# A one-scalar minimum on GpSimd, written with a second scalar

## The chip, the core and the metric

The kernel runs on one core of one Trainium2 chip. The metric is the device time of one execution in microseconds (us), as the median of several runs. Engines are named as in the profile: PE is TensorE's matmuls, PEld its weight loads, DVE VectorE, ACT ScalarE, POOL GpSimd, SP SyncE (here the queue that issues nearly all DMAs).

## What is computed

A chain of three layers in float32, on 4 batches of 576 tokens:

1. attention of 8 heads of width 64, mixed by a gate with a lookup in a memory matrix:

```python
scores = q @ k.T / 8, causal;  local = softmax(scores) @ v
phi(x) = where(x > 0, x, exp(x) - 1.0) + 1.0
mem_out = (phi(q) @ M_prev) / (phi(q) @ z_prev + 1e-6)
x = g * mem_out + (1 - g) * local          # g = sigmoid(beta), per head
```

2. `x @ w_in`, then `h - tanh(h)`, then `@ w_out` (512 to 2048 to 512), over 2304 tokens;
3. a second such layer (512 to 1024 to 512) with softmax and a layer norm between its two products.

The change lies in `phi`, the feature map. The kernel computes it as max(x + 1, exp(min(x, 0))), which is the same function.

## The kernel before

The program has three stages on one time axis. **Attention** works on 16 pairs of heads (`p` = 0 to 15), from the start to about 200 us. **Moe1** is the second item above, in eight slices of 256 hidden columns by five blocks of tokens, to about 580 us. **Moe2** is the third, in 18 tiles of 128 tokens, to the end.

The order of the attention stage is written out by hand. A table of text (`PROLOGUE` for the first pairs, then `PERIOD` with two halves, one for each parity of `p`) names one small step after another, as `f_neg:-1:p` for "step `f_neg`, of the pair one behind, on GpSimd". `run` issues them in just this order, and each engine executes its own steps in the order of issue. An engine whose next step has to wait stands still, with all that is queued behind it. Two pairs of heads thus take one turn of the table.

The steps that the prediction speaks of, by line:

- `q_t`, `k_t` (L248), DVE: transposes of q and k. They wait for the q and k loads on SP's queue (L187).
- `f_neg` (L263), POOL: `e` = min(qT, 0), a tile of 128 partitions by 576 elements, two buffers. Its input is the transposed q.
- `f_exp` (L266), ACT: exponential of `e`; `f_max` (L270), DVE: max(qT + 1, `e`), which makes `f`.
- `m_mm` (L282), PE: `f` times the memory matrix, into `R`; `m_mul` (L301), DVE: `R` divided, into `xm`.
- `s_r` (L326) and `s_l` (L342), PE: scores `S` and, for the last 64 rows of two pairs together, `S_L`; `s_max` (L356), DVE; `s_exp` (L383), ACT: the exponentials `P` and `PL` and their sums `sm`.
- `s_eps` (L395), POOL: 1e-9 added to a few sums, one scalar; `s_inv` (L399), DVE: their reciprocals.
- `s_norm` (L410), POOL: each block of `P` and `PL` times its reciprocal and the gate, two scalars taken from memory.
- `a_t` (L450), PE: transposes `T` of the blocks of `P`, and last in a turn those of `PL` (the shared last rows); `a_ev` (L457), ACT, copies them out; `a_mem` (L432) and `a_pv` (L477), PE: the products with v, `X`.
- between them, POOL also prepares the next stage: `split_x` (L675), from pair 4 on, and the conversion of weights (L887, L896).

In Moe1, L890 on POOL is one more operation of two scalars: a product with a value from memory, and a product with the constant 1.0.

The step that the change touches, and what runs the table:

Of the kernel before, what the change touches and what calls it, by code (L numbers as in the profile page):

```python
# [13 lines left out]
ALU = mybir.AluOpType  # L14
# [17 lines left out]
class Attention:  # L32
# [227 lines left out]

    def f_neg(self, p):
        e = self.e[p] = self.sp.tile([P, self.S], F32, tag="fe", name=f"e{p}", bufs=2)
        self.eng.tensor_scalar_min(e, self.QT[p], 0.0)  # L263

    def f_exp(self, p):
        self.nc.scalar.activation(self.e[p], self.e[p], AF.Exp)  # L266
# [1043 lines left out]
```

## Time and profile before

| | |
|---|---|
| median of 3 runs | 788.77 us (788.38 to 789.33) |
| the profiled execution's own time | 789.29 us |
| its span, first to last instruction | 787.5 us |
| PE, share of the span | 99% |
| DVE, POOL, ACT | 72%, 48%, 44% |
| granted TensorE clock | full in all 40 slices of the span |

The profile shows one execution. Its span is 1.8 us shorter than its own time. Busy PE is modelled (matmuls overlap, and their ends are reckoned), so 99% tells little of whether PE waited; what the text uses are starts of groups of matmuls on the time axis, and the waits of the weight loads ahead of them.

### The profile page before, as it was taken

The numbers are of one execution on the slowest core, as the hardware profiler recorded it, in microseconds if no ns is written. First come the engines' busy times: TensorE is split into PE (matmuls) and PEld (weight loads), VectorE is DVE, ScalarE is ACT, GpSimd is POOL, SyncE is SP. The second block draws the span as 40 slices with busy tenths as digits, with TensorE's granted clock in tenths as the row PEclk, the third lists the DMA queues.
The fourth block names the chain that finished last, engine by engine and source line by source line (L and its number), as shares of the span: only waits on it lengthen the run. The fifth ranks groups of instructions, "written<-read, shape, count | busy, mean of one in ns | idle before, by whom it ended". The sixth has DMA issues, their size and how long they took to land.

```text
span 787.5 us, 12510 instructions
## 1 busy us (share of the span) xinstructions
PE 777.2 (99%) x4532; PEld 645.9 (82%) x4532; DVE 567.7 (72%) x1064; ACT 348.5 (44%) x692; POOL 379.8 (48%) x386
## 2 busy tenths in 40 slices
PE   8999999999999999999999999999999999999998
PEld 6777677777798898988989889898898888888887
DVE  5899888983477786776877776777877766566661
ACT  4889899994243243242332422233322333323321
POOL 6788999986223342333333333334532443334421
PEclk9999999999999999999999999999999999999999
DMA  7677877651002221211212111112100344333341
GB/s 181 150 192 160 164 145 163 139 121 58 0 28 81 64 71 54 81 54 54 81 54 80 54 54 54 54 54 81 55 28 30 123 146 143 110 118 111 131 134 55
DMA packets 77119, 73.04 MB, mean 93 GB/s; under 512 B 51072, under 2 KB 60032, under 8 KB 77056
## 3 DMA queue, kind: packets, MB, share of 16 engines
q1 hardware_dynamic: 76896, 71.93, 34.0%
q8 instruction: 36, 0.59, 0.3%
q10 hardware_dynamic: 160, 0.30, 0.2%
q14 instruction: 27, 0.22, 0.1%
HBM read 54.38 MB, written 13.11 MB: 86 GB/s over the span
## 4 chain that ended last, share of the span: by engine, by line
PE 74%; DMA 1%; ACT 0%; DVE 0%; SPq 0%; issue 0%; ACTq 0%
PE Y L739 25%; PE H L707 24%; PE H L933 12%; PE O16X L1027 1%; PE O15S L1027 1%; PE O14X L1027 1%; PE O13X L1027 1%; PE O12X L1027 1%; PE O11X L1027 1%; PE O10X L1027 1%; PE O9X L1027 1%; PE O8X L1027 1%; PE O7X L1027 1%; PE O6X L1027 1%; PE O5X L1027 1%; PE O4X L1027 1%
## 5 line engine op out<-in xcount | busy, mean ns | idle before, releaser
L739 PE MATMUL Y<-G,wo 128*128 128x512 f32 (+1 forms) x960 | 204.8, 368 | 0.9 <-DVE G L724 0.6
L739 PEld LDWEIGHTS Y<-G,wo 128*128 128x128 f32 x960 | 174.6, 188 | 25.9 <-issue 1.6
L707 PE MATMUL H<-xh,wi 128*128 128x512 f32 (+1 forms) x640 | 151.6, 369 | 0.0
L887 POOL TENSOR_TENSOR raw<-raw,cva 128x512 f32<-128x512 f32 x48 | 63.0, 1313 | 174.6 <-DVE cva L885 161.0
L707 PEld LDWEIGHTS H<-xh,wi 128*128 128x128 f32 x640 | 117.1, 188 | 15.8 <-issue 0.4
L721 ACT ACTIVATE t<-H 128x1024 f32<-128x1024 f32 (+1 forms) x40 | 37.6, 941 | 136.6 <-PE H L707 135.2
L933 PE MATMUL H<-w2i,Ys 128*128 128x512 f32 x384 | 89.6, 389 | 0.0
L707 PE MATMUL H<-xT,wi 128*128 128x512 f32 (+1 forms) x320 | 84.6, 368 | 0.0
L933 PEld LDWEIGHTS H<-w2i,Ys 128*128 128x128 f32 x384 | 72.0, 188 | 14.9
L410 POOL TENSOR_SCALAR P<-P,sm,og 128x512 f32<-128x512 f32 (+3 forms) x124 | 82.0, 676 | 3.0 <-DVE n L292 0.8
L753 DVE TENSOR_TENSOR yT<-Y,yT 128x512 f32<-128x512 f32 (+3 forms) x105 | 77.3, 789 | 1.3 <-PE Y L739 1.2
L724 DVE TENSOR_TENSOR G<-t,G 128x1024 fp32r<-128x1024 f32 (+1 forms) x40 | 45.6, 1139 | 42.3 <-ACT G L723 42.3
L723 ACT CAST G<-t 128x1024 fp32r<-128x1024 f32 (+1 forms) x40 | 38.6, 966 | 84.1 <-DVE t L722 84.1
L383 ACT ACTIVATE P<-P,mx 128x384 f32<-128x384 f32 (+3 forms) x128 | 71.1, 557 | 8.2 <-DVE mx L356 8.1
L722 DVE TENSOR_TENSOR t<-H,t 128x1024 f32<-128x1024 f32 (+1 forms) x40 | 44.6, 1115 | 33.6 <-ACT t L721 33.5
L950 ACT ACTIVATE e<-H,s 128x1024 f32<-128x1024 f32 x18 | 20.1, 1118 | 109.2 <-DVE s L944 109.2
L1279 POOL TENSOR_TENSOR Ys<-yT,Ys 128x512 fp32r<-128x512 f32 x16 | 20.7, 1296 | 93.2 <-ACT Ys L1278 80.7
L707 PEld LDWEIGHTS H<-xT,wi 128*128 128x128 f32 x320 | 58.8, 188 | 7.6
L356 DVE CUSTOM_DVE_ANT_0 P<-S,mask 128x384 f32<-128x384 f32 (+3 forms) x128 | 55.8, 484 | 7.0 <-PE S L326 6.9
L457 ACT COPY pt<-T 128x512 f32<-128x512 f32 (+1 forms) x95 | 53.7, 604 | 12.2 <-PE T L450 11.8
L477 PE MATMUL X<-pt,v 128*64 128x64 f32 (+4 forms) x576 | 47.3, 318 | 0.0
L994 POOL TENSOR_TENSOR L<-rest,L 128x1024 fp32r<-128x1024 f32 x16 | 38.7, 2421 | 16.0 <-ACT L L993 8.8
(162 smaller groups left out, 1219.7 us busy)
## 6 DMA issues: line engine op xcount, KB each, us to landing
raw<-in_moe_w_in_dram SPq DMA_DIRECT2D x24, 512.0 KB, 3.8
raw<-in_moe_w_out_dram SPq DMA_DIRECT2D x16, 512.0 KB, 3.3
D<-rest SPq DMA_DIRECT2D x16, 512.0 KB, 2.6
rest<-D SPq DMA_DIRECT2D x64, 128.0 KB, 3.0
q<-in_q_dram SPq DMA_DIRECT2D x56, 140.0 KB, 3.3
out_dram<-ob SPq DMA_DIRECT2D x17, 256.0 KB, 3.0
v<-in_v_dram SPq DMA_DIRECT2D x32, 128.0 KB, 3.9
raw<-in_moe_w_out_dram SPq DMA_DIRECT2D x32, 128.0 KB, 2.7
```

The source lines that it names most:

```text
L356: self.nc.vector.tensor_tensor_reduce(out=self._block(p, i), in0=s, in1=mask, scale=-0.125, scalar=3.0e38, op0=ALU.add, op1=ALU.min, accum ...
L383: self.nc.scalar.activation(t, t, AF.Exp, bias=self.mx[p][:, i : i + 1], scale=-1.0, accum_out=self.sm[p][:, i : i + 1],)
L410: eng.tensor_scalar(d, d, self.sm[p][:, i : i + 1], og, ALU.mult, ALU.mult)
L457: self.copy(pt, T)
L477: self.nc.tensor.matmul(self.X[j * D : (j + 1) * D, q0 : q0 + w], v[:, kb, j, :], pt[:, o : o + w], start=False, stop=False, skip_group_ch ...
L707: nc.tensor.matmul(H[a:z, f], wi[:, wl, c, f * P + a : f * P + z], self.x[n][xl][:, c], start=(count[f] == 0), stop=(count[f] == 3 * KD - ...
L724: nc.vector.tensor_tensor(G[:, 1], t, G[:, 0].bitcast(F32), ALU.subtract)
L739: nc.tensor.matmul(Y[d][:, 0:NB], wo[:, wl, f, d * P : (d + 1) * P], G[:, gl, f], start=(i == 0), stop=(i == 3 * KF - 1),)
L753: nc.vector.tensor_tensor(y, src, y, ALU.add)
L887: self.eng.tensor_tensor(w, w, a, ALU.add)
L933: nc.tensor.matmul(H[:, nh * 512 : (nh + 1) * 512], Y[:, yl, c, :], w2i[:, wl, c, nh * 512 : (nh + 1) * 512], start=(k == 0), stop=(k == 3 ...
L1027: nc.tensor.matmul(O[n][:, 0:w], L[:, ll, f, :], self.w2o[f][:, wl, a : a + w], start=(k == 0), stop=(k == len(order) - 1),)
```

## The change

The minimum of `f_neg` gets a second operation: the result of the minimum with 0.0 is multiplied by 1.0 in the same instruction. The values are the same. No instruction is added, removed or moved on any engine or queue.

```diff
     def f_neg(self, p):
         e = self.e[p] = self.sp.tile([P, self.S], F32, tag="fe", name=f"e{p}", bufs=2)
-        self.eng.tensor_scalar_min(e, self.QT[p], 0.0)
+        self.eng.tensor_scalar(e, self.QT[p], 0.0, 1.0, ALU.min, ALU.mult)
```

## Rows read from the trace of the kernel before

**Rows 1.** The page, part 1: busy time of each engine, share of the span, instructions.

```profile
PE 777.2 (99%) x4532; PEld 645.9 (82%) x4532; DVE 567.7 (72%) x1064; ACT 348.5 (44%) x692; POOL 379.8 (48%) x386
```

**Rows 2.** Chain that ended last, in order of time: start us, us, what.

```profile
200.85 10.25 PE Y L739 x44
...
784.52 0.37 ACT ob L1032
```

**Rows 3.** Busy us by stretch: PE, PEld, DVE, ACT, POOL; clock, DMA.

```profile
100.00:120.00 20.00, 19.92 (x190) 13.98 (x189) 17.76 (x56) 19.02 (x51) 19.47 (x26) 1.00 0.79 148
```

**Rows 4.** Timeline of POOL: start us, us, instruction [idle before <- releaser].

```profile
69.16 0.23 POOL L395 TENSOR_SCALAR sm<-sm 128x6 f32<-128x6 f32 x1 [0.95 <-ACT P L383]
...
99.01 0.23 POOL L395 TENSOR_SCALAR sm<-sm 128x2 f32<-128x2 f32 x1 [0.16 <-ACT P L383]
...
166.73 0.24 POOL L395 TENSOR_SCALAR sm<-sm 128x6 f32<-128x6 f32 x1 [0.99 <-ACT P L383]
```

**Rows 5.** Line 263: durations ns min/median/max, first and last start us; who waited (nobody).

```profile
L263 POOL TENSOR_SCALAR e<-qT x16: 1640/1652/1807, 8.7 to 164.1; 128x576 f32<-128x576 f32 x16
...
who waited for it (us, times):
```

**Rows 6.** The same for 69 to 167 us alone.

```profile
L263 POOL TENSOR_SCALAR e<-qT x10: 1640/1652/1807, 69.5 to 164.1; 128x576 f32<-128x576 f32 x10
```

**Rows 7.** Timeline of PE, the turn of the table from 37 us.

```profile
37.46 1.20 PE L342 MATMUL S_L<-kT,qT 64*64 64x512 f32 x16
...
47.59 0.60 PE L450 MATMUL T<-ident,P 128*128 128x128 f32 x4
48.03 1.25 PE L450 MATMUL T<-ident,PL 128*128 128x128 f32 x10
...
58.46 1.26 PE L342 MATMUL S_L<-kT,qT 64*64 64x512 f32 x16
```

**Rows 8.** Timeline of PE, the four turns from 79 to 167 us.

```profile
79.69 1.25 PE L342 MATMUL S_L<-kT,qT 64*64 64x512 f32 x16
...
89.86 0.60 PE L450 MATMUL T<-ident,P 128*128 128x128 f32 x4
91.03 0.77 PE L450 MATMUL T<-ident,PL 128*128 128x128 f32 x5 [0.57 <-POOL PL L410]
92.10 0.77 PE L450 MATMUL T<-ident,PL 128*128 128x128 f32 x5 [0.30 <-DVE xm L301]
...
166.98 1.20 PE L342 MATMUL S_L<-kT,qT 64*64 64x512 f32 x16
```

**Rows 9.** Waits from 79 to 167 us: us in total, times, longest.

```profile
PEld T L450 <- POOL PL L410: 2.2, 4, 0.8
...
DVE qT L248 <- DMA q<-in_q_dram: 2.0, 2, 1.7
PEld T L450 <- POOL P L410: 1.8, 5, 0.4
...
PE T L450 <- POOL PL L410: 1.1, 2, 0.6
```

**Rows 10.** Timeline of the weight loads: two of their waits.

```profile
44.13 0.86 PEld L450 LDWEIGHTS T<-ident,P 128*128 128x128 f32 x8 [0.39 <-POOL sm L395]
...
141.80 0.74 PEld L450 LDWEIGHTS T<-ident,P 128*128 128x128 f32 x7 [0.27 <-POOL P L410]
```

**Rows 11.** POOL by line and shape: count | busy us, mean ns | idle before.

```profile
L410 POOL TENSOR_SCALAR P<-P,sm,og 128x256 f32<-128x256 f32 x31 | 17.7, 574 | 0.0
...
L410 POOL TENSOR_SCALAR PL<-PL,sm,ogL 128x576 f32<-128x576 f32 x15 | 12.5, 841 | 0.5 <-DVE sm L399 0.3 <-PE T L450 0.2
...
L890 POOL TENSOR_SCALAR raw<-raw,gl 128x512 f32<-128x512 f32 x8 | 5.9, 732 | 0.8
```

**Rows 12.** Line 395, two single instructions: durations ns min/median/max.

```profile
L395 POOL TENSOR_SCALAR sm<-sm x1: 233/233/233, 120.3 to 120.3; 128x2 f32<-128x2 f32 x1
...
L395 POOL TENSOR_SCALAR sm<-sm x1: 236/236/236, 134.9 to 134.9; 128x6 f32<-128x6 f32 x1
```

## The prediction

> **What bounds the kernel now.** The busy times come first [rows 1]: PE 99%, POOL 48%. An operation on POOL seems far from mattering. The chain that ended last says more on where to look [rows 2]: from 200.85 us to the last copy at 784.52 us it is PE alone, matmul after matmul. So whatever makes the attention stage end sooner or later moves the end by as much, and nothing that POOL does behind 200 us counts here. For the attention stage itself I read the busy times by stretch and the time axis of each engine.
>
> There POOL looks different. From 100 to 120 us it is busy 19.47 of 20 us [rows 3], and between its idle piece at 69.16 us and that at 166.73 us its queue stood idle once, for 0.16 us [rows 4]. For nearly 100 us POOL is a queue with no slack, in a stage whose other engines are full too (PE 19.92, ACT 19.02, DVE 17.76 of 20).
>
> How much of that reaches PE is read from one turn of the hand-written order to the next, two pairs of heads each. The turn from 37.46 to 58.46 us, ahead of that long stretch, took 21.00 us on PE [rows 7]. The four turns from 79.69 to 166.98 us took 87.29 us [rows 8], 3.29 us more than four times 21.00. The clearest place is the transposes of `PL`: they begin 0.44 us after the group ahead of them in the undisturbed turn [rows 7], and 1.17 us after it in the turn at 90 us, released by POOL's `PL` [rows 8]. So PE is the bound of this stage, POOL stands right behind it, and PE loses something under 3.3 us to a late POOL.
>
> **The change, part by part.** Nothing moves: the same instructions in the same order, with the same waits. Only the duration of 16 instructions changes, those of line 263, now 1652 ns at the median [rows 5].
>
> *Price of the new instruction.* The trace has no minimum with two scalars, so it is bounded by neighbours. The nearest row is the operation of the same class and shape with two scalars, `s_norm` on `PL`: 841 ns for 128 by 576, just half [rows 11]. Line 890 has one of its two scalars as the constant 1.0, as here, and takes 732 ns for 512 elements, 1.43 ns each, which makes 0.82 us for 576. That is the low end. For the high end the second operation could cost a second pass at the present pace: (1652 - 233) / 574 = 2.47 ns for each element, with the 233 ns of a two-element operation as the fixed part [rows 5, 12], so 576 x 2.47 = 1.42 us more, 3.07 us in all. I take 0.83 us, since both rows that share the form (two scalars, this engine, this width) lie there, and the one row of full width with one scalar is the slow one. A saving of 0.82 us each, 13.1 us over the 16.
>
> The Trainium skill's GPSIMD Engine Reference, section "Elementwise — side-by-side cycle accounting", says that a loop body of up to two operations for each element runs at 1.03 cycles per element, bound by its ports; with the 1.2 GHz of its specifications that makes an estimate of 0.49 us for the 576 elements, in either form. By that rule the change would bring nothing. The trace does not bear it out for the present form, whose pace is 2.47 ns per element, nearly three times the page's.
>
> *What lies beside other work.* Nobody waits for `f_neg` [rows 5]: its consumer `f_exp` comes later anyway. So its own latency is worth nothing, and only the queue behind it counts. Ahead of 69.16 us POOL waited 0.95 us for ACT, and a shorter `f_neg` before that point only lengthens the wait; the same holds at 166.73 us, where POOL idles 0.99 us [rows 4]. So of the 13.1 us only the ten operations between matter, 8.2 us [rows 6], and these only up to what PE now loses.
>
> *What PE gets back.* Its weight loads wait for POOL's `PL` 2.2 us in these four turns, in 4 pieces [rows 9]. The first shortened `f_neg` of the stretch, at 69.5 us [rows 6], makes POOL's queue 0.82 us earlier, as much as the longest of these waits (0.8), and each later one as much again, so all of it should go: 2.2 us. The waits for POOL's `P` are 1.8 us in 5 pieces. Four of them are 0.39 us or just under, and the same pause of 0.39 us stands at 44.13 us, in the turn of 21.00 us [rows 10]: I take these as cover for matmuls still running, worth nothing. The fifth, 0.27 us at 141.80 us, I count as 0.3. Sum: 2.2 + 0.3 = 2.5 us. Low end: only the 1.1 us in which PE itself is shown idle [rows 9]. High end: the full 3.29 us, with the 0.3 us wait at 92.10 us for `xm` [rows 8] and small delays of single steps included. That `xm` was late because DVE's transpose of q waited 1.7 us for its load [rows 9], and I see no reason that POOL caused this.
>
> *What is late next.* PE itself. Its turn of 21.00 us is above what POOL would need (19.47 of 20 us means some 21.2 us of the average 21.8 us turn; less 1.65, 19.6 us) and above ACT's (19.02 of 20, some 20.7 us). So the saving on POOL beyond 3.3 us goes into POOL's waiting. The end of the stage, with its fixed path from `x` by DMA to Moe1, shifts as a whole.
>
> The profiled execution took 789.29 us, which gives 786.8; against the median of 788.77 us, 0.5 us lower, it is **786.3 us**. That is 0.3% less. No change means within 0.2%, 1.6 us, about what a measurement of this kernel can tell.
>
> **Rivals.**
>
> *The price stays (0.19).* The slow part is the minimum, not the form: the only full-width one-scalar row is also the only minimum. For this speaks line 395, an addition with one scalar: four more elements cost it only 3 ns, 0.8 ns each [rows 12], a fast pace, though so few elements prove little. Against it stand only neighbours of another operation. Or the factor 1.0 is folded away when the instruction is made, and nothing changes at all (0.03 of the 0.19). Time: 788.8 us. The Trainium skill's rule above would end here too, by another road: with one pace for both forms.
>
> *The second operation costs extra (0.17), slower.* If the minimum keeps its pace and the product comes on top, it costs at least one more operation for each element. The step from 256 to 576 elements of `s_norm` costs (841 - 574) / 320 = 0.83 ns per element [rows 11], so 576 elements 0.48 us. The place is POOL's queue from 69 to 167 us: ten of the 16 `f_neg` start there [rows 6], and only 0.16 us of idle time is left to hide in [rows 4], so nearly all reaches PE through the late `PL`: 10 x 0.48 - 0.2 = 4.6 us, 793.4 us. It decides from 0.18 us per instruction on, as ten of these less 0.2 make 1.6 us. With the high price of 1.42 us it would be near 803 us.
>
> *Fast, but PE does not follow (part of the forecast's 0.64).* If just the 1.1 us of PE's own idle time comes back, the end is 787.7 us, inside no change.
>
> **How the numbers follow.** The forecast has 0.64; within it 0.54 for more than 1.6 us gained and 0.10 for less. The constant price has 0.19, of which 0.18 stays within 0.2% and 0.01 falls on the slower side. The dearer operation has 0.17, 0.16 of it slower by over 1.6 us. So faster 0.54, same 0.29, slower 0.17. The forecast's own range is 785.3 to 787.7 us (3.3 to 1.1 us gained, and 0.2 for the spread of a median). The range given runs from 785.0, for a little more than PE's whole loss, to 791.5, which holds the constant price and the mild part of the dearer one (up to 0.29 us each); what is left out is some 0.15.
>
> **What would show it.** In the changed kernel line 263 stands near 0.83 us. POOL has idle pieces again between 70 and 166 us, mostly ahead of line 395, waiting for ACT. The four waits of the weight loads for `PL` are gone, a turn on PE takes 21.0 to 21.2 us, and the group of `S_L` that started at 166.98 us starts near 164.5 us. After 200 us all is as before, earlier by the same amount. It is wrong if line 263 keeps or exceeds 1652 ns (price), or if it falls and the turns still take 21.8 us (then PE waited for something that only looked like POOL).

## The result, and the profile after

The changed kernel takes 793.65 us (793.3 to 794.11, 4 runs), the kernel before in the same comparison 789.05 us. The ratio is 1.0058, with a 95% interval of 1.0045 to 1.007: slower by 4.6 us. The forecast was 786.3 us, with a range up to 791.5, so the time lies outside it. The rival that the prediction had given 0.17, a second operation that costs extra, had 793.4 us.

The price decides it. Line 263 in the changed kernel (durations in ns, minimum, median, maximum; who waited for it):

```profile
L263 POOL TENSOR_SCALAR e<-qT x16: 2132/2145/2168, 8.4 to 167.6; 128x576 f32<-128x576 f32 x16
...
who waited for it (us, times):
  ACT e L266: 2.6, 6
```

Before it was 1652 ns, and nobody waited [rows 5]. The product comes on top: 493 ns for 576 elements, 0.86 ns each.

The page's busy times, and the chain that ended last (start us, us, what):

```profile
PE 777.6 (98%) x4532; PEld 644.9 (81%) x4532; DVE 568.8 (72%) x1064; ACT 349.3 (44%) x692; POOL 386.7 (49%) x386
```

```profile
204.68 10.31 PE Y L739 x44
```

PE is as busy as before [rows 1], POOL has 6.9 us more (line 263 alone 34.3 us against 26.6, which is 7.7 more, less 0.8 in other lines). The unbroken work of PE starts at 204.68 us, not at 200.85 [rows 2]: 3.8 us later. All of it was lost in the attention stage. There, on POOL's time axis:

```profile
69.03 0.23 POOL L395 TENSOR_SCALAR sm<-sm 128x6 f32<-128x6 f32 x1 [0.96 <-ACT P L383]
...
170.28 0.24 POOL L395 TENSOR_SCALAR sm<-sm 128x6 f32<-128x6 f32 x1 [0.50 <-ACT P L383]
```

The two idle pieces that frame the long stretch were at 69.16 and 166.73 us [rows 4]. Now there is none between them, and the stretch is 3.7 us longer. On PE:

```profile
37.10 1.20 PE L342 MATMUL S_L<-kT,qT 64*64 64x512 f32 x16
...
80.02 1.20 PE L342 MATMUL S_L<-kT,qT 64*64 64x512 f32 x16
...
90.32 0.60 PE L450 MATMUL T<-ident,P 128*128 128x128 f32 x4
92.03 1.31 PE L450 MATMUL T<-ident,PL 128*128 128x128 f32 x10 [1.10 <-POOL PL L410]
...
99.19 0.98 PE L450 MATMUL T<-ident,P 128*128 128x128 f32 x7 [0.35 <-POOL P L410]
...
170.53 1.20 PE L342 MATMUL S_L<-kT,qT 64*64 64x512 f32 x16
```

The four turns take 90.51 us, against 87.29 [rows 8] and a floor of 84.0. The transposes of `PL` now begin 1.71 us after the group ahead of them, where it was 1.17 before and 0.44 undisturbed [rows 7, 8]. The waits from 79 to 172 us say who was late (us in total, times, longest):

```profile
DVE sm L399 <- POOL sm L395: 5.4, 7, 1.3
...
PEld T L450 <- POOL PL L410: 3.5, 4, 1.3
...
PEld T L450 <- POOL P L410: 2.9, 6, 0.5
...
PE T L450 <- POOL PL L410: 2.4, 3, 1.1
...
ACT e L266 <- POOL e L263: 1.8, 4, 0.5
...
PE T L450 <- POOL P L410: 1.3, 4, 0.4
...
PE S L326 <- DVE mx L356: 0.6, 2, 0.3
```

PE's own idle time behind POOL went from 1.1 us [rows 9] to 3.7 (2.4 and 1.3). The 0.6 us behind DVE's `mx` are new too, and both pieces (at 105.44 and 150.65 us) also go back to POOL: DVE had stood waiting 0.93 us for sums that POOL finished right behind an `f_neg` of 2.15 us, and worked without a pause from there to `mx`. The first:

```profile
103.93 0.19 DVE L399 RECIPROCAL sm<-sm 128x6 f32<-128x6 f32 x1 [0.93 <-POOL sm L395]
```

### The profile page after: what moved, and what is told of

It is laid out like the page before. It is cut to its first block, busy times and chain, and to the rows that moved or that the text cites. A ratio compares the mean times of both kernels' runs of the same rounds, so it can differ in the third digit from the quotient of the medians.

```text
span 791.4 us, 12510 instructions
## 1 busy us (share of the span) xinstructions
PE 777.6 (98%) x4532; PEld 644.9 (81%) x4532; DVE 568.8 (72%) x1064; ACT 349.3 (44%) x692; POOL 386.7 (49%) x386
## 4 chain that ended last, share of the span: by engine, by line
PE 74%; DMA 1%; ACT 0%; DVE 0%; SPq 0%; issue 0%; ACTq 0%
PE Y L739 25%; PE H L707 24%; PE H L933 12%; PE O16X L1027 1%; PE O15S L1027 1%; PE O14X L1027 1%; PE O13X L1027 1%; PE O12X L1027 1%; PE O11X L1027 1%; PE O10X L1027 1%; PE O9X L1027 1%; PE O8X L1027 1%; PE O7X L1027 1%; PE O6X L1027 1%; PE O5X L1027 1%; PE O4X L1027 1%
## 5 line engine op out<-in xcount | busy, mean ns | idle before, releaser
L450 PE MATMUL T<-ident,P 128*128 128x128 f32 x320 | 46.0, 277 | 2.0 <-POOL P L410 1.8
```

The lines of the kernel that those rows point to most:

```text
L450: nc.tensor.transpose(T[:, P * i : P * i + P], t, self.ident)
```

## The experiments

Edits are against the kernel before, unless said otherwise. Three questions were open. What makes a GpSimd operation of this class cheap or dear? Do only the ten operations behind 69 us count? And would the forecast have held, had the operation become cheap?

### Prices, first list

Twelve kinds of operation, each twice, on a scratch tile in Moe2's tiles 4 to 15, one kind in each:

```diff
+        if i == 3:
+            x = tp.tile([P, 2048], F32, tag="G", name="probe", bufs=2)
+            nc.vector.memset(x, 0.5)
+        if 3 < i < 16:
+            probe(nc, x, i - 4, 640)
+            probe(nc, x, i - 4, 1280)
...
+    if k == 1:
+        t.tensor_scalar(o, a, 0.0, 1.0, ALU.min, ALU.mult)
```

> The kernel before, with one-off operations on GpSimd added in Moe2's tiles (two of each kind, 128x576 on a scratch tile, where GpSimd has room), to read prices. Theory A (each operation has its own pace per element and they add up; the minimum is the dear one): a minimum alone 1.65 us, minimum then product 2.15, a product alone or an addition alone 0.7 to 0.8, two products 0.8, product then minimum 2.15, minimum with scalars from memory as dear as with constants; half the width of the minimum 0.94 us. Theory B (constants as scalars are dear, values from memory cheap): two products with constants 2 us or more, two products with scalars from memory 0.84, minimum and product with scalars from memory 0.84. Theory C (the form with one scalar is dear as such): product alone 1.65 us, addition alone 1.65. The time itself should stay at that of the kernel before, within 0.2%.

Line 263 stayed at 1652 ns, and the one time taken was 790.14 us. Durations of the added lines (ns, minimum, median, maximum). In order: minimum; minimum then product; product; two products; addition; addition then product; maximum; product then minimum; two products, minimum then product, both with scalars from memory; minimum at half the width; minimum then maximum:

```profile
L1288 POOL TENSOR_SCALAR probe<-probe x2: 1644/1690/1737, 634.3 to 636.0; 128x576 f32<-128x576 f32 x2
L1290 POOL TENSOR_SCALAR probe<-probe x2: 2133/2134/2136, 644.0 to 646.2; 128x576 f32<-128x576 f32 x2
L1292 POOL TENSOR_SCALAR probe<-probe x2: 1650/1702/1753, 653.7 to 655.4; 128x576 f32<-128x576 f32 x2
L1294 POOL TENSOR_SCALAR probe<-probe x2: 677/894/1111, 663.4 to 664.0; 128x576 f32<-128x576 f32 x2
L1296 POOL TENSOR_SCALAR probe<-probe x2: 1661/1704/1747, 673.1 to 674.8; 128x576 f32<-128x576 f32 x2
L1298 POOL TENSOR_SCALAR probe<-probe x2: 684/900/1117, 682.7 to 683.4; 128x576 f32<-128x576 f32 x2
L1300 POOL TENSOR_SCALAR probe<-probe x2: 1647/1689/1731, 693.5 to 695.2; 128x576 f32<-128x576 f32 x2
L1302 POOL TENSOR_SCALAR probe<-probe x2: 2142/2153/2164, 704.4 to 706.6; 128x576 f32<-128x576 f32 x2
L1304 POOL TENSOR_SCALAR probe<-probe x2: 836/1052/1268, 715.3 to 716.1; 128x576 f32<-128x576 f32 x2
L1306 POOL TENSOR_SCALAR probe<-probe x2: 2292/2297/2302, 726.2 to 728.5; 128x576 f32<-128x576 f32 x2
L1308 POOL TENSOR_SCALAR probe<-probe x2: 922/1090/1257, 737.1 to 738.3; 128x288 f32<-128x288 f32 x2
L1310 POOL TENSOR_SCALAR probe<-probe x2: 669/886/1103, 748.0 to 748.6; 128x576 f32<-128x576 f32 x2
```

I read the shorter of each two: with it the first two lines agree with line 263 in its own place (1652 and 2145 ns). In the lines that take some 0.68 us, the second of the two took 0.43 us longer than the first; what lengthens it was not tried.

Theories A and B fall, and C holds half. A single operation costs 1.64 to 1.66 us whatever it is (minimum, product, addition, maximum), so the minimum is not special and the form with one scalar is dear as such. But a second scalar makes it cheap only for some pairs: two products 0.68, addition then product 0.68, minimum then maximum 0.67. A minimum and a product, in either order, are the dear 2.13 to 2.14. Scalars from memory instead of constants add 0.16 us to two products and to minimum then product, and do not decide which is dear.

### Prices, second list

The same, with twelve other lines in `probe`. The one time taken was 790.05 us.

> A second list of prices, read as in the first. Theory D: a pair of two operations of one kind (products, sums and differences among each other; minimum and maximum among each other) is fast, 0.67 to 0.69 us for 576 elements; anything else, a single operation or a pair across the two kinds, runs at 2.45 ns for each element, with 0.85 ns more for the second operation. So minimum twice 0.67, addition twice 0.68, product then addition 0.68, subtraction then product 0.68, addition then maximum 2.14, maximum then product 2.14, maximum then addition 2.14, a single minimum with its scalar from memory 1.7, minimum with maximum from memory 0.84, minimum then product at half the width 1.2, minimum then maximum at half the width 0.45. Theory E: what is slow is only the constant 0 or 1.0 in a particular place or the minimum ahead of a product; then maximum then addition and addition then maximum are fast as well.

In order of line: minimum twice; addition twice; addition then maximum; product then addition; maximum then product; maximum then addition; subtraction then product; a single minimum with its scalar from memory; and at half the width minimum then product, and minimum then maximum. Two lines that are not shown were a plain copy (660 ns) and minimum then maximum with scalars from memory (814 ns), both at full width:

```profile
L1288 POOL TENSOR_SCALAR probe<-probe x2: 2132/2148/2163, 634.1 to 636.2; 128x576 f32<-128x576 f32 x2
L1290 POOL TENSOR_SCALAR probe<-probe x2: 2145/2161/2177, 643.8 to 646.0; 128x576 f32<-128x576 f32 x2
L1292 POOL TENSOR_SCALAR probe<-probe x2: 2144/2148/2152, 653.5 to 655.6; 128x576 f32<-128x576 f32 x2
L1294 POOL TENSOR_SCALAR probe<-probe x2: 691/904/1117, 663.1 to 663.8; 128x576 f32<-128x576 f32 x2
L1296 POOL TENSOR_SCALAR probe<-probe x2: 2147/2156/2166, 672.8 to 674.9; 128x576 f32<-128x576 f32 x2
L1298 POOL TENSOR_SCALAR probe<-probe x2: 2141/2144/2147, 682.5 to 684.6; 128x576 f32<-128x576 f32 x2
L1300 POOL TENSOR_SCALAR probe<-probe x2: 2152/2157/2162, 693.4 to 695.5; 128x576 f32<-128x576 f32 x2
L1302 POOL TENSOR_SCALAR probe<-probe x2: 1716/1758/1799, 704.3 to 706.1; 128x576 f32<-128x576 f32 x2
L1304 POOL TENSOR_SCALAR probe<-probe x2: 1172/1215/1258, 715.2 to 716.4; 128x288 f32<-128x288 f32 x2
L1306 POOL TENSOR_SCALAR probe<-probe x2: 427/644/862, 726.1 to 726.5; 128x288 f32<-128x288 f32 x2
```

Theory D was wrong for three of its pairs, and E for both of its own. Minimum twice, addition twice and subtraction then product are dear; product then addition is cheap. So it is no rule of kinds but particular pairs: of those tried, product with product, addition with product, product with addition, and minimum with maximum. Everything else that was tried is dear. From half to full width, the cheap pair costs (669 - 427) / 288 = 0.84 ns per element, a dear pair (2133 - 1172) / 288 = 3.34, a single operation (1644 - 922) / 288 = 2.51. Why just these pairs are cheap, no run shows.

### The dear operation early, and late

```diff
-        self.eng.tensor_scalar_min(e, self.QT[p], 0.0)
+        if p < 6:
+            self.eng.tensor_scalar(e, self.QT[p], 0.0, 1.0, ALU.min, ALU.mult)
+        else:
+            self.eng.tensor_scalar_min(e, self.QT[p], 0.0)
```

> The changed operation for pairs 0 to 5 only, the one of before for the ten that start behind 69 us. If only those ten count, because GpSimd waits for ScalarE ahead of 69 us anyway: the time of the kernel before within 0.2%, line 263 at 2.15 us six times and 1.65 us ten times. Rival: every dearer operation counts alike, 6 of 16 of the loss, some 1.7 us more.

788.75 us against 788.59, a ratio of 1.0004 (0.9995 to 1.0013). Line 263 has become two lines in this kernel, L264 for the early pairs and L266 for the others (1650 ns at the median), and PE's `S_L` stands on L345:

```profile
L264 POOL TENSOR_SCALAR e<-qT x6: 2132/2144/2166, 8.6 to 56.5; 128x576 f32<-128x576 f32 x6
```

```profile
80.39 1.25 PE L345 MATMUL S_L<-kT,qT 64*64 64x512 f32 x16
...
166.91 1.20 PE L345 MATMUL S_L<-kT,qT 64*64 64x512 f32 x16
```

Six operations at 2144 ns cost nothing that can be measured: the interval ends at 1.0 us, below the 1.7 us of the rival. The four turns took 86.52 us with the same operations in them as before, where the trace of before has 87.29 [rows 8]. In the runs of the two lists, also unchanged in this stretch, they took 87.18 and 86.55 us. So the profiled execution of before is at the slow end here, by up to 0.8 us.

The mirror has `p > 5` in the condition.

> The mirror of the fourth run: the changed operation for pairs 6 to 15 only, the ten that start behind 69 us, and the one of before for pairs 0 to 5. If only those ten count: the whole loss, 4 to 5 us more than before, as in the changed kernel. Rival, every one counts alike: 10 of 16 of it, 2.9 us more.

793.68 us against 788.85, a ratio of 1.006 (1.0046 to 1.0073): the whole loss. That is 4.8 us for ten operations that are 0.5 us longer (2148 ns at the median). It shows that the place in the order decides, and that in this stretch POOL hands the delay on to PE nearly one to one.

### The cheap operation, and none

Both kernels leave out the minimum of the feature map. The first has a cheap operation in its place:

```diff
-        self.eng.tensor_scalar_min(e, self.QT[p], 0.0)
+        self.eng.tensor_scalar(e, self.QT[p], 1.0, 1.0, ALU.mult, ALU.mult)
```

> The two-scalar form with two products by 1.0 in place of the minimum (left out: the minimum of the feature map). Theory A: line 263 takes 0.7 to 0.85 us. Then this is the cheap operation that the prediction had counted on, and its working gives 2.5 us less than the kernel before (1.1 to 3.3 us): the four waits for PL are gone and a turn on PE takes 21.0 to 21.2 us. Rival: POOL was not what PE waited for, and the time stays within 0.2% of before. Theory B: line 263 takes 2 us or more and the time is 4 us longer or more.

Line 263 took 672 ns, and the kernel 787.76 us against 788.59: a ratio of 0.9991 (0.9982 to 1.0). A gain of 0.8 us, with none just inside the interval, and not 2.5. The time alone would also fit the rival, that PE did not wait for POOL. The late run speaks against it, and so does this trace: from 79 to 167 us the weight loads wait for `PL` 1.0 us in 2 pieces, where it was 2.2 us in 4 [rows 9].

The second has no operation on POOL at all:

```diff
-        self.eng.tensor_scalar_min(e, self.QT[p], 0.0)
+        pass
...
-        self.nc.scalar.activation(self.e[p], self.e[p], AF.Exp)
+        self.nc.scalar.activation(self.e[p], self.QT[p], AF.Exp)
```

> No minimum at all: line 263 is left out, and the exponential reads the transposed q itself (left out: the minimum of the feature map). POOL loses 1.65 us for each pair of heads. If PE is the bound behind POOL, this gains no more than the cheap operation of the second run, 2.5 to 3.5 us against before, though twice as much work is gone. If POOL is still the bound at 0.83 us, it gains about twice as much as that run.

788.02 us, a ratio of 0.9991 (0.9982 to 1.0), the same. Leaving the work out altogether brings no more that can be measured than making it cheap, so from some 0.7 us down the length of the operation no longer shows in the time. Its four turns on PE, from 80.57 to 166.18 us, took 85.61 us.

### A cheap pair that keeps the minimum

```diff
-        self.eng.tensor_scalar_min(e, self.QT[p], 0.0)
+        self.eng.tensor_scalar(e, self.QT[p], 0.0, -3.0e38, ALU.min, ALU.max)
```

> The kernel before with the minimum paired with a second operation of its own kind: minimum with 0, then maximum with -3e38, which leaves every value as it is. If the price hangs on the pair (minimum with maximum fast, minimum with product slow), line 263 takes 0.67 us and the time is that of the second run, 0.8 us less than before (0 to 1.5). Rival: the price of 0.67 us held only in Moe2, where the row was read; then line 263 takes 1.65 us or more, and the time is that of before or longer.

787.69 us against 788.85, a ratio of 0.9988 (0.9979 to 0.9996): faster than both kernels, by 1.2 us against before and some 6 against the changed one. Line 263 in its own place:

```profile
L263 POOL TENSOR_SCALAR e<-qT x16: 658/668/864, 8.5 to 162.2; 128x576 f32<-128x576 f32 x16
```

Where the saved time went is seen on POOL's and PE's time axes in one turn:

```profile
76.12 0.23 POOL L395 TENSOR_SCALAR sm<-sm 128x2 f32<-128x2 f32 x1 [0.92 <-ACT P L383]
79.24 0.24 POOL L395 TENSOR_SCALAR sm<-sm 128x6 f32<-128x6 f32 x1 [0.90 <-ACT P L383]
79.96 0.77 POOL L410 TENSOR_SCALAR P<-P,sm,og 128x512 f32<-128x512 f32 x1 [0.49 <-DVE sm L399]
```

```profile
87.97 1.28 POOL L675 TENSOR_TENSOR xT<-xT,xh 128x512 fp32r<-128x512 f32 x1
89.23 1.63 POOL L410 TENSOR_SCALAR PL<-PL,sm,ogL 128x576 f32<-128x576 f32 x2
```

```profile
79.49 1.47 PE L342 MATMUL S_L<-kT,qT 64*64 64x512 f32 x16
...
90.05 0.60 PE L450 MATMUL T<-ident,P 128*128 128x128 f32 x4
90.91 1.31 PE L450 MATMUL T<-ident,PL 128*128 128x128 f32 x10 [0.26 <-POOL PL L410]
...
165.14 1.20 PE L342 MATMUL S_L<-kT,qT 64*64 64x512 f32 x16
```

The two `f_neg` ahead of this turn's `PL`, 0.98 us shorter each, give POOL 2 us, and POOL at once waits 2.3 us for ACT and DVE, in the three idle pieces from 76 to 80 us. From there to `PL` it works 11 us without a pause and without any `f_neg` among it, so `PL` is still late. The step to it fell from 1.17 us [rows 8] only to 0.86. In all the four turns took 85.65 us, 1.64 less than in the trace of before and 0.87 less than in that of the early run. Not all that is left above 21.00 us is POOL's: in this turn the group ahead of `PL` begins 10.56 us after the turn's start, where it was 10.13 in the undisturbed turn [rows 7]. What delays it by 0.43 us was not followed.

### The split of x behind `PL`

The run with minimum and maximum, and in the table:

```diff
-        a_pv:-4:-:2 s_norm:-3:-:6 x_ev:-4:v s_exp:-2:-:2 a_t:-3:-:3 a_ev:-3:a:3 room:0:-:2
+        a_pv:-4:-:2 s_norm:-3:-:6 x_ev:-4:v s_exp:-2:-:2 a_t:-3:-:3 a_ev:-3:a:3
...
-        s_exp:-2:-:5 a_t:-3:-:0 m_eps:-2:- s_norm:-2:-:8 a_ev:-3:a:0 m_inv:-2:- a_t:-3:-:4
+        s_exp:-2:-:5 a_t:-3:-:0 m_eps:-2:- s_norm:-2:-:8 room:0:-:2 a_ev:-3:a:0 m_inv:-2:- a_t:-3:-:4
```

> As the run with minimum and maximum, and one entry of the table moved: the split of x for Moe1 (line 675) that stands ahead of the two products of PL on GpSimd now stands behind them. The waits of the weight loads for PL that stay at 0.25 us even where line 263 is left out come from this 1.3 us ahead of PL in the queue, if GpSimd is what is late there; then they go, worth up to 0.3 us in each of two turns, 0.5 us less than with minimum and maximum alone. Rival: the waits only change their place (the split is late for ScalarE's next cast, or PL waits for its sums), and the time stays within 0.3 us of that run.

788.14 us against 788.85, a ratio of 0.9991 (0.9983 to 1.0), not to be told from the run without the move (787.69). The first part of the expectation came true, the waits for `PL` went, and the second, the gain, did not. The rival named the mechanism; its limit of 0.3 us between the two medians was missed by 0.15, less than the runs of either kernel spread. In the turn at 91 us:

```profile
90.55 0.60 PE L450 MATMUL T<-ident,P 128*128 128x128 f32 x4
90.99 1.25 PE L450 MATMUL T<-ident,PL 128*128 128x128 f32 x10
...
97.98 0.98 PE L450 MATMUL T<-ident,P 128*128 128x128 f32 x7 [0.23 <-POOL P L410]
```

The step to `PL` is the undisturbed 0.44 us, and 7 us later PE waits for a block of `P` instead. Here the wait changed its place.

## Why the prediction was wrong

*What bounds the kernel.* Right, and shown: PE, with POOL right behind it from 69 to 167 us. The early and the late run show it from the slow side.

*The price of the new instruction.* This step failed, and with it the sign. The prediction took 0.83 us from two rows that "share the form (two scalars, this engine, this width)". The lists show that the number of scalars is not what sets the price but the pair of operations: the two rows were both two products [rows 11], one of the few cheap pairs. It measured 2145 ns. What the prediction had as the nearest row was near in shape and far in what mattered. Its reading of the slow side was good: 1652 ns is the price of any single operation, and the rival's 0.48 us for a product on top, from the slope of line 410, measured 0.49.

*The slower rival* holds in price, place (the ten behind 69 us) and sum (4.6 us foretold, 4.6 measured, 4.8 with the ten alone). Its road was drawn too narrow: `PL` is only 2.4 of PE's 3.7 us of idle time behind POOL, the other 1.3 are blocks of `P`. That the sum agrees to 0.1 us is partly luck, as a median of this kernel before moved by 0.5 us between comparisons (788.59 to 789.05). It had 0.17, because the rows for the fast form looked like two witnesses and were one.

*The rival of the constant price* leaned on line 395, whose four further elements cost 3 ns [rows 12]; at 2.51 ns each they should cost 10. So few elements said nothing, as the text had allowed.

The Trainium skill's GPSIMD Engine Reference, section "Elementwise — side-by-side cycle accounting", gives 1.03 cycles per element for bodies of up to two operations. With the 1.2 GHz of its section "Specifications" that makes an estimate of 0.86 ns. The cheap pairs run at 0.84 ns, as it says; the single operations at 2.51 and the other pairs at 3.34 do not, so by the measurement its rule holds here for some pairs only.

*What PE gets back* was mis-sized as well: 2.5 us forecast for a cheap operation, 0.8 (0 to 1.4) and 1.2 us (0.3 to 1.7) measured with two of them. The prediction's own low end, 1.1 us, lies inside both intervals. The step that failed is the sentence that each later `f_neg` makes POOL's queue "as much again" earlier. POOL gives the time back in waits for ACT and DVE (with minimum and maximum it waits 8.2 us for ACT from 79 to 167 us, where it was 1.2 before), so savings do not add up along the queue, whereas delays do. Two of the four waits for `PL` went, and the other two fell only from 0.8 to 0.5 us. The floor of four times 21.00 us was not reached even with line 263 left out (85.61 us). Also, the 3.29 us that PE seemed to lose were read from one execution. By the traces of the early run and of the two lists, unchanged in this stretch, the four turns lose 2.5 to 3.2 us against 84.0. The profiled execution held a late q load (1.7 us on DVE) [rows 9] that the trace of the early run shows with 0.2 us, and its own time of 789.29 us is 0.7 above the median of 788.59 that 27 runs of that kernel gave. The late load is not what makes the stretch slow: the first list's run took its 87.18 us without one. What does is open.

## What to carry to other kernels

Measure the exact pair of operations of a GpSimd `tensor_scalar`, not its form. For 128 by 576 float32 elements with constants as scalars, product and product, addition and product, product and addition, minimum and maximum took 0.67 to 0.69 us, where the single operations and the other pairs tried took 1.64 to 2.15. The minimum here could be written as one of the cheap pairs (minimum with 0, then maximum with -3e38). On POOL's queue, full and just behind the bound, delays added up and savings did not: price a slower step in such a place at its full sum, and a faster one only up to the next wait of that queue. The six slower steps that lay where POOL waits anyway cost nothing measurable.

## What was not expected

A plain copy of 576 elements took 660 ns on GpSimd and minimum with maximum 668, while a single minimum took 1652: two operations took 0.4 of the time of one. Minimum twice (2132 ns) and minimum then maximum (669 ns) differ by a factor of 3.2.
